# Attention, a gated mixture of experts and a second feed-forward on one core: scatters bound to their steps, ranks behind the next scores, the branch inside the last expert

## The chip, the cores and the metric

The kernel runs on one core of a Trainium2 chip. The metric is the device time of the whole program in microseconds; before the change three runs gave 991.46, 991.9 and 992.49 us. Engines go by the profile's names: PE is TensorE (PEld its weight loads), DVE VectorE, ACT ScalarE, POOL GpSimd, SP SyncE. Each has its own instruction queue and takes it in order; they wait for each other on semaphores.

## What is computed

Three stages in a row, all in float32. First, causal attention in a window of 128 with a linear bias, for 4 batches of 8 heads, 576 positions, head size 64:

```
scores = where(0 <= rel < 128, q @ k.T / 8 - slope[h] * |rel|, -1e9)
attn   = exp(scores - max) / (sum + 1e-9);   x = attn @ v        # 2304 tokens x 512
```

Second, a mixture of 8 experts (512 to 1024 to 512), each token sent to the two with the highest noisy gate value, weighted by a softmax over the two:

```
noisy = x @ w_gate + log1p(exp(x @ w_noise)) * noise;   top2, weights = best two, softmax
out[token] += weight * (relu(x[token] @ w1[e]) @ w2[e])
```

Third, a dense feed-forward on all tokens: `(relu(x @ w_in) ** 2) @ w_out`, 512 to 2048 to 512.

## The kernel before

**Attention.** The 2304 tokens are 18 tiles of 128, the 8 heads two halves: 36 steps. The loop over v (L549 on) runs the scores of step v + 2 (`s_step`), transposes the probabilities of v + 1 (`t_step`) and multiplies by the values for v (`pv_step`, then `norm`). Behind the scores DVE makes four row reductions (L259, each with a read-out of the row maximum, tile mx), then ACT the exponentials. Scores and value products alternate in the two PSUM buffers named b, so a new step's scores wait until the four reductions of the step before have read theirs. Buffer c, of which there is one, is shared by the gate's transposes (L330), its products (L341, L349), the ranks (L384) and some later work.

**The gate, folded in.** Pairs of tiles p = 0 to 8 are gated while attention goes on. A table `todo`, filled by `at(v, slot, f)`, says beside which step and at which place of it a piece runs: slots 0 to 3 stand behind the four reductions of L259, slot 4 behind the transposes, slot 5 behind the value products. For a pair, `gate_t` transposes its tokens, `gate_w` and `gate_m` make the logits, `gate_o` picks the top two (L360 to L374), `rank` counts on PE how many tokens before this one chose the same expert (one-hot times a triangle, plus the running count acc), `place` turns that into a slot number (its first piece is the CAST of L394, which reads the ranks from buffer c), and `scatter` writes token numbers into a table of slots by an indirect DMA on POOL, four to a pair, with a small POOL instruction (the spacer, L424) ahead of each. Three early parts of the table are read by SP (`early_table`, L498) as soon as all tokens that can belong to them are placed; `gather` (L438) then fetches the tokens by an indirect DMA, and `x_in` (L445) transposes them for the first expert, all before attention ends.

**Experts.** Eight experts in a row, each: first layer in two parts (`mm1_a`, 384 columns, and `mm1_b`, 256), second layer `mm2` in five tiles of 128 rows (L787). fp32 products are split into three passes. Weights come through `raw` buffers and are split by ACT, DVE and POOL. Where a token would not fit in its expert's slots, the count `most` is above zero and a slow general path `fallback` is run behind a `tc.If` (L989), which stands between the seventh and the last expert. It isn't taken for these inputs. Each engine reads the flag and branches by itself.

**Behind the last expert.** While it works, sums of second-stage weights are made (L868), and the expert outputs of each token are fetched (`ygather`, L707), weighted and added (`combine`, L713 and L714), and transposed (`x2_in`, L723). A table C_AT says beside which f of the last `mm1_a` they stand, M_AT beside which (j, f) of the last second layer. Then L1040 and L1195 are the dense feed-forward.

## Time and profile before

| | us |
|---|---|
| median of 3 runs (lowest, highest) | 991.9 (991.46, 992.49) |
| the profiled execution | 989.7 |
| its span, first to last instruction | 987.8 |
| PE busy in it | 961.7 |
| DVE, ACT, POOL busy | 672.1, 463.8, 419.0 |

The profile follows one execution. A timeline lists what an engine did with start and duration; matmuls overlap, so one starts before the last has ended, and the distance from start to start says what one costs. In brackets stands the idle time ahead of a row and what ended it. "Granted clock" is PE's clock as a share of full speed; over the whole span it is 0.995.

### The profile page before, as it was taken

The page shows a single profiled execution, that of the slowest core. Times are in us where ns is not written, and L with a number is a line of the kernel's source. Part 1 is how long each engine was busy: PE and PEld are TensorE (multiplying, and loading weights), DVE is VectorE, ACT ScalarE, POOL GpSimd, SP SyncE. Part 2 cuts the span into 40 slices and gives each one's busy share as a digit, 9 for nine tenths or more (in the row PEclk, how much of TensorE's full clock was granted, in tenths as well). Part 3 has the DMA queues.
Part 4 walks back from the last instruction along what each step waited for, and adds up shares of the span by engine and source line. Part 5 has one row for each costly group of instructions (what it writes and reads, how often), then busy time and mean ns, then how long its engine had stood idle before and what let it go on. Part 6 is the DMA issues. An engine that isn't in the chain of part 4 may idle for free. (4 is left out here: it accounts for less than half of the span.)

```text
span 987.8 us, 19656 instructions
## 1 busy us (share of the span) xinstructions
PE 961.7 (97%) x7452; PEld 882.1 (89%) x7452; DVE 672.1 (68%) x1424; ACT 463.8 (47%) x887; POOL 419.0 (42%) x453
## 2 busy tenths in 40 slices
PE   8998999999999999999999799999999999999998
PEld 5776779898998989899898797999999998999998
DVE  4777754657585776857584235778577899877773
ACT  5777743334343433434243336665555564433331
POOL 1564553124233323515243023624212657988880
PEclk9999999999999999999999899999999999999999
DMA  9767625456667575656655352975637874444331
GB/s 324 261 220 265 205 88 153 131 167 224 204 211 225 176 238 199 219 188 215 217 191 171 112 160 87 293 216 168 168 105 211 237 219 139 150 146 132 129 107 43
DMA packets 118199, 180.70 MB, mean 183 GB/s; under 512 B 11104, under 2 KB 66032, under 8 KB 117712
## 3 DMA queue, kind: packets, MB, share of 16 engines
q1 hardware_dynamic: 107120, 147.46, 46.3%
q0 software_dynamic: 10976, 31.90, 10.5%
q8 instruction: 60, 0.98, 0.4%
q14 instruction: 43, 0.35, 0.1%
HBM read 125.02 MB, written 54.30 MB: 182 GB/s over the span
## 5 line engine op out<-in xcount | busy, mean ns | idle before, releaser
L868 POOL TENSOR_TENSOR gs<-xb 128x256 f32<-128x256 f32 x72 | 69.2, 982 | 28.2 <-DVE wc L868 12.6
L473 ACT ACTIVATE ha<-psa 128x384 fp32r<-128x384 f32 x64 | 31.3, 490 | 93.7 <-PE psa L469 92.2
L265 ACT ACTIVATE p<-p,mx 128x192 f32<-128x192 f32 x144 | 57.6, 451 | 31.1 <-DVE mx L259 30.2
L707 POOL DMA_INDIRECT yr<-yg,pos x36 | 36.5, 1012 | 76.5 <-DVE ha L474 50.9
L686 POOL TENSOR_TENSOR et<-ex,et 128x512 f32<-128x512 f32 x16 | 20.8, 1301 | 111.9 <-DVE ex L682 111.9
L474 DVE SCALAR_TENSOR_TENSOR ha<-psa,ha 128x384 fp32r<-128x384 f32 x64 | 35.4, 553 | 46.5 <-ACT ha L473 46.4
L259 DVE CUSTOM_DVE_ANT_0 p<-psb,bias 128x192 f32<-128x192 f32 x144 | 45.8, 352 | 15.6 <-PE psb L254 14.5
L425 POOL DMA_INDIRECT slots<-tok,pos x36 | 35.0, 972 | 44.8 <-DVE rs L311 32.6
L438 POOL DMA_INDIRECT xr<-xd,gidx x40 | 44.7, 1118 | 21.4 <-issue 6.7
L469 PE MATMUL psa<-xa,wa 128*128 128x384 f32 x288 | 53.4, 336 | 0.1
L469 PE MATMUL psa<-xa,wc 128*128 128x384 f32 x288 | 53.1, 335 | 0.0
L787 PE MATMUL psb<-wa,ha 128*128 128x512 f32 x216 | 53.1, 396 | 0.0
L791 ACT ACTIVATE yo<-psb 128x512 f32<-128x512 f32 x38 | 22.7, 597 | 60.5 <-PE psb L787 46.3
L469 PEld LDWEIGHTS psa<-xa,wa 128*128 128x128 f32 x288 | 49.4, 188 | 0.4 <-DVE ha L474 0.3
L469 PEld LDWEIGHTS psa<-xa,wc 128*128 128x128 f32 x288 | 49.6, 188 | 0.2
L868 DVE TENSOR_TENSOR wc<-gs,wc 128x512 fp32r<-128x512 f32 x48 | 48.5, 1050 | 0.0
L882 POOL DMA_DIRECT2D raw<-w x49 | 27.3, 562 | 49.8 <-DVE wb L868 18.4
L686 POOL TENSOR_TENSOR ex<-ex 128x512 f32<-128x512 f32 x12 | 15.6, 1301 | 75.4 <-DVE ex L682 75.4
L787 PEld LDWEIGHTS psb<-wa,ha 128*128 128x128 f32 x216 | 39.5, 188 | 7.8
L787 PE MATMUL psb<-wb,ha 128*128 128x512 f32 x176 | 46.3, 398 | 0.0
L110 DVE TENSOR_TENSOR wa<-raw,wa 128x1024 fp32r<-128x1024 f32 x20 | 25.6, 1279 | 29.6 <-ACT wa L106 29.6
L469 PE MATMUL psa<-xb,wc 128*128 128x256 f32 x288 | 39.6, 294 | 5.2 <-DVEq L989 5.2
(326 smaller groups left out, 2738.2 us busy)
## 6 DMA issues: line engine op xcount, KB each, us to landing
raw<-in_w_dram SPq DMA_DIRECT2D x64, 512.0 KB, 5.0
xb<-gmid SPq DMA_DIRECT2D x72, 256.0 KB, 2.8
v<-in_vt_dram SPq DMA_DIRECT2D x20, 520.0 KB, 4.7
yg<-yo SPq DMA_DIRECT2D x40, 256.0 KB, 3.4
raw<-w POOLq DMA_DIRECT2D x36, 256.0 KB, 3.6
gmid<-yo SPq DMA_DIRECT2D x48, 192.0 KB, 2.7
ex<-in_w_in_dram SPq DMA_DIRECT2D x16, 512.0 KB, 4.1
ex<-in_w_out_dram SPq DMA_DIRECT2D x16, 512.0 KB, 3.6
```

The costliest lines, as they stand in the source:

```text
L259: nc.vector.tensor_tensor_reduce(out=p2[j][:, a, :], in0=ps[:, a, j, :], in1=bias[:, 4 * g + 2 * j + a, :], op0=OP.add, op1=OP.min, scale= ...
L265: nc.scalar.activation(out=p2[j][:, a, :], in_=p2[j][:, a, :], func=AF.Exp, bias=mx[j][:, a:a + 1], scale=-1.0)
L425: st = nc.gpsimd.indirect_dma_start(out=slots, out_offset=bass.IndirectOffsetOnAxis(ap=pos[:, i, k:k + 1], axis=0), in_=tok[:, i:i + 1], i ...
L438: nc.gpsimd.indirect_dma_start(out=XR[e, j], out_offset=None, in_=xd[0:PARTS[j] * 128] if early else xd, in_offset=bass.IndirectOffsetOnAx ...
L469: nc.tensor.matmul(o, w[wp][:, f * 128:(f + 1) * 128], x[:, xp, d, :], start=(n == 0), stop=(n == 11))
L473: nc.scalar.activation(out=hi, in_=ps, func=AF.Relu)
L474: nc.vector.scalar_tensor_tensor(out=lo, in0=ps, scalar=0.0, in1=hi.bitcast(F32), op0=OP.max, op1=OP.subtract)
L686: nc.gpsimd.tensor_tensor(out=x, in0=af, in1=cf, op=OP.add)
L707: nc.gpsimd.indirect_dma_start(out=YR[i, k], out_offset=None, in_=yg, in_offset=bass.IndirectOffsetOnAxis(ap=pos[:, i, k:k + 1], axis=0))
L787: nc.tensor.matmul(py, h[:, hq], wc[wp][:, wsl], start=(f + n == 0), stop=(f == 7 and n == 2))
L868: f(**a)
L882: (nc.sync if m < 15 else nc.gpsimd).dma_start(out=w_buf(m)[:, 0:256 * n_i], in_=w7[kk, :, i:i + n_i, :].rearrange("p i n -> p (i n)"))
```

## The change

- `scatter`: the spacer instruction is now a copy of one element of mx, the row maximum of the step in which it is issued, so it waits for that step's last reduction. Scatters stand one to a step in four steps, two to a step for the late pairs, and all four together for the last pair; before, two to a step in two steps.
- `rank`: from slot 5 of its step to a new slot 6 of the next step, which stands behind that step's score products and ahead of its reductions. `place` is spread over two steps instead of one.
- Early rows: `early_table`, `gather` and `x_in` of the three parts stand at steps 19/20/24, 27/28/32 and 33/34/36, where they stood at 17/18/20, 25/26/28 and 31/32/36; the gather stands in slot 2 instead of 5.
- The branch: from between the last two experts to a place inside the last expert's second layer, behind the first 12 of its 120 products; the path that isn't taken uses other scratch.
- `combine`, `x2_in` and `ygather` of the first three tiles each stand one f earlier.

```diff
--- before.py
+++ after.py
@@ -227,7 +227,7 @@
 
     def s_step(v, now):
         if v >= NV:
-            for n in range(4):
+            for n in (6, 0, 1, 2, 3):
                 run(now, n)
             return
         i, g = divmod(v, 2)
@@ -254,11 +254,13 @@
                     nc.tensor.matmul(ps[64 * x:64 * x + 64, a, j, 192 - n:192],
                                      Q[i][pa, 2 * g + j, 64 * x:64 * x + 64], K[b][pa, 2 * g + j, k0:k0 + n],
                                      start=True, stop=True)
+        run(now, 6)
         for j in range(2):
             for a in range(2):
                 nc.vector.tensor_tensor_reduce(
                     out=p2[j][:, a, :], in0=ps[:, a, j, :], in1=bias[:, 4 * g + 2 * j + a, :],
                     op0=OP.add, op1=OP.min, scale=-0.125, scalar=3.0e38, accum_out=mx[j][:, a:a + 1])
+                G["mx"] = mx[j]
                 run(now, 2 * j + a)
         for j in range(2):
             for a in range(2):
@@ -419,9 +421,9 @@
             nc.vector.tensor_tensor(out=pos[:, two, :], in0=pf, in1=over, op=OP.min)
             del G["gs", p], G["oh", p], G["ri", p]
 
-    def scatter(i):
-        for k in range(2):
-            nc.gpsimd.memset(spacer, 0.0)
+    def scatter(i, *ks):
+        for k in ks:
+            nc.gpsimd.tensor_copy(spacer, G["mx"][0:1, 1:2])
             st = nc.gpsimd.indirect_dma_start(
                 out=slots, out_offset=bass.IndirectOffsetOnAxis(ap=pos[:, i, k:k + 1], axis=0),
                 in_=tok[:, i:i + 1], in_offset=None)
@@ -519,19 +521,18 @@
         o = v + 2 if end else v + 3
         for n, c in enumerate((0, 0, 0, 1, 2)):
             at(o, c, gate_o, p, n)
-        at(o, 4 if end else 5, rank, p)
-        for n, c in enumerate((0, 1, 1, 2, 2, 3)):
-            at(o + 1, c, place, p, n)
-        at(o + 1, 3, scatter, 2 * p)
-        if end or 2 * p + 2 == PARTS[-1]:
-            at(o + 1, 4, scatter, 2 * p + 1)
-        else:
-            at(o + 2, 3, scatter, 2 * p + 1)
+        at(o + 1 - end, 4 if end else 6, rank, p)
+        q = o + (1 if end else 2)
+        for n, c in enumerate((0, 1, 1, 2, 2, 3) if end else (-3, -1, 0, 1, 1, 2)):
+            at(q - (c < 0), c % 4, place, p, n)
+        per = 4 if end else 2 if 2 * p + 2 >= PARTS[-1] else 1
+        for n in range(4):
+            at(q + n // per, 4 if end and n > 1 else 3, scatter, 2 * p + n // 2, n % 2)
     at(0, 3, more_consts)
     at(4, 4, zero_rows)
-    for j, (v, w, x) in enumerate(((17, 18, 20), (25, 26, 28), (2 * PARTS[-1] + 3, 2 * PARTS[-1] + 4, last + 1))):
+    for j, (v, w, x) in enumerate(((19, 20, 24), (27, 28, 32), (2 * PARTS[-1] + 5, 2 * PARTS[-1] + 6, last + 1))):
         at(v, 4, early_table, j)
-        at(w, 5, gather, 0, j, True)
+        at(w, 2, gather, 0, j, True)
         at(x, 5, x_in, 0, j)
     at(last, 5, keep_warm, 24)
     at(last + 2, 3, mm1_a, 0, 0)
@@ -725,8 +726,9 @@
 
 
     def fallback():
-        wb, wt, ex = lay("wb", F32), lay("wt", F32), lay("ex", F32)
-        w = [(wb[:, m * 1024:(m + 1) * 1024], wb[:, (m + 4) * 1024:(m + 5) * 1024] if m < 3 else wt) for m in range(4)]
+        ha, xb, ex = lay("ha", F32), lay("xb", F32), lay("ex", F32)
+        w = [(ha[:, m * 1024:(m + 1) * 1024], ha[:, (m + 4) * 1024:(m + 5) * 1024] if m < 2 else
+              xb[:, (m - 2) * 1024:(m - 1) * 1024]) for m in range(4)]
         xs = ex[:, 0:3072]
         xr, hf = xs[:, 0:512], xs[:, 1024:2048].rearrange("p (f n) -> p f n", f=8)
         xt, yf = xs[:, 512:1024].rearrange("p (c n) -> p c n", c=4), xs[:, 2048:2560]
@@ -985,9 +987,6 @@
                 if j < 4 and nprep[0] < 8 * (e + 1) + 8:
                     prep_one()
 
-    settle("rest")
-    with tc.If(nc.values_load(most[0:1, 0:1], min_val=0, max_val=N) > 0):
-        fallback()
     settle("wb")
     wq = [f for n in range(3) for f in w_sums(n, 0)]
     for f in range(8):
@@ -1003,6 +1002,11 @@
     for j in range(2):
         py = bank("b")[:, 0, :] if j else bank("c")
         for f in range(8):
+            if (j, f) == (0, 4):
+                with tc.If(nc.values_load(most[0:1, 0:1], min_val=0, max_val=N) > 0):
+                    fallback()
+                big["ha"] = lay("ha")
+                settle("rest")
             mm2(last, j, f, py)
             if len(wq) > 8:
                 wq.pop(0)()
@@ -1010,8 +1014,8 @@
     settle("xb")
     for i in range(3):
         ygather(i)
-    C_AT = {5: [(combine, 0)], 6: [(x2_in, 0, "b"), (ygather, 3), (combine, 1)],
-            7: [(x2_in, 1, "b"), (ygather, 4), (combine, 2)]}
+    C_AT = {4: [(combine, 0)], 5: [(x2_in, 0, "b"), (ygather, 3), (combine, 1)],
+            6: [(x2_in, 1, "b"), (ygather, 4), (combine, 2)], 7: [(x2_in, 2), (ygather, 5)]}
     for f in range(8):
         mm1_a(last, f)
         out_a(last, f)
@@ -1019,7 +1023,7 @@
             g(*a)
         wq.pop(0)()
     settle("wc")
-    M_AT = {0: [(x2_in, 2), (ygather, 5)], 1: [(combine, 3)], 2: [(x_hi, 0)], 3: [(x2_in, 3), (x_lo, 0, "dve")], 4: [(combine, 4)], 5: [(x_hi, 1)],
+    M_AT = {1: [(combine, 3)], 2: [(x_hi, 0)], 3: [(x2_in, 3), (x_lo, 0, "dve")], 4: [(combine, 4)], 5: [(x_hi, 1)],
             6: [(x2_in, 4), (x_lo, 1, "dve")], 8: [(combine, 5)], 10: [(x2_in, 5)], 11: [(x_early, 6)],
             12: [(x_early, 5)], 13: [(x_hi, 5)], 14: [(x_early, 3), (x_lo, 5, "dve")], 15: [(x_hi, 3)],
             16: [(x_lo, 3, "dve"), (x_hi, 6)], 17: [(x_early, 4), (x_lo, 6, "dve")], 19: [(x_hi, 4)],
```

PE in attention, pair 2: the products of L300 (values), L384 (ranks), L254 (scores), L276 and L330 (transposes) of one step. Before:

```order
L300 MATMUL psb<-v,pt 64x65 x16
L384 LDWEIGHTS tri
L384 MATMUL psc<-oh,tri 128x8
...
L384 MATMUL psc<-acc,ones 128x8
L254 MATMUL psb<-k,q 64x192 x8
L276 MATMUL psa<-cst,p_1206 128x128 x3
L276 MATMUL psa<-cst,p_1212 128x128 x3
L330 MATMUL psc<-cst,xi 128x128 x4
```

And now, with lines two higher:

```order
L302 MATMUL psb<-v,pt 64x65 x16
L254 MATMUL psb<-k,q 64x192 x8
L386 LDWEIGHTS tri
L386 MATMUL psc<-oh,tri 128x8
...
L386 MATMUL psc<-acc,ones 128x8
L278 MATMUL psa<-cst,p_1202 128x128 x3
L278 MATMUL psa<-cst,p_1208 128x128 x3
L332 MATMUL psc<-cst,xi 128x128 x4
```

The ranks went from ahead of the scores to behind them; everything else of the step keeps its place.

DVE in the same step, from the last part of `norm` on: xi is the attention output, acc the running count, L394 (now L396) the cast that reads the ranks, the L259 pairs (now L260) the reductions. Before:

```order
L317 TENSOR_TENSOR xi<-psb,rs 128x256
L387 TENSOR_TENSOR acc<-acc,oh 128x16 x2
L259 ISA p_1287,mx<-psb,bias 128x192
L259 ISA mx 128x1
L394 CAST ri<-psc 128x16
L259 ISA p_1287,mx<-psb,bias 128x192
L259 ISA mx 128x1
L398 TENSOR_SCALAR ri<-ri 128x16
```

And now:

```order
L319 TENSOR_TENSOR xi<-psb,rs 128x256
L389 TENSOR_TENSOR acc<-acc,oh 128x16 x2
L260 ISA p_1272,mx<-psb,bias 128x192
L260 ISA mx 128x1
L260 ISA p_1272,mx<-psb,bias 128x192
L260 ISA mx 128x1
L396 CAST ri<-psc 128x16
L260 ISA p_1278,mx<-psb,bias 128x192
```

The cast stands behind the second reduction instead of the first, and the rest of `place` went behind the fourth and into the next step.

PE at the branch, which is the pair TENSOR_LOAD and COMPARE_AND_BRANCH (L989, now L1006); wb and wt hold weights of the seventh expert, wa and wc of the last. Before:

```order
L787 MATMUL psb<-wb,hb 128x512 x2
L787 MATMUL psb<-wt,hb 128x512
L787 MATMUL psb<-wb,hb 128x512
L989 TENSOR_LOAD most
L989 COMPARE_AND_BRANCH
...
L989 UNCONDITIONAL_BRANCH x2
L469 MATMUL psa<-xb,wc 128x256 x96
L787 MATMUL psc<-wa,hb 128x512 x24
```

And now:

```order
L789 MATMUL psb<-wb,hb 128x512
L471 MATMUL psa<-xb,wc 128x256 x96
L789 MATMUL psc<-wa,hb 128x512 x12
L1006 TENSOR_LOAD most
L1006 COMPARE_AND_BRANCH
...
L1006 UNCONDITIONAL_BRANCH x2
L789 MATMUL psc<-wa,hb 128x512 x12
L789 MATMUL psb<-wa,hb 128x512 x24
```

The branch went behind the 96 products of the last expert's first layer and the first half of a chain of 24 of its second.

## Rows read from the trace of the kernel before

**Rows 1.** The page's first part: busy time of each engine and its share.

```profile
PE 961.7 (97%) x7452; PEld 882.1 (89%) x7452; DVE 672.1 (68%) x1424; ACT 463.8 (47%) x887; POOL 419.0 (42%) x453
```

**Rows 2.** Timeline of PE, 12 to 66 us: start, duration, instructions, idle before.

```profile
12.08 1.56 PE L254 MATMUL psb<-k,q 64*64 64x192 f32 x16 [2.23 <-DMA q<-in_qt_dram]
...
53.74 1.13 PE L300 MATMUL psb<-v,pt 128*64 128x65 f32 x32
54.69 0.83 PE L254 MATMUL psb<-k,q 64*64 64x192 f32 x16
...
61.48 0.21 PE L384 MATMUL psc<-oh,tri 128*128 128x8 bf16 x2 [0.31 <-DVE oh L372]
...
61.92 0.88 PE L254 MATMUL psb<-k,q 64*64 64x192 f32 x16
...
63.46 0.63 PE L330 MATMUL psc<-cst,xi 128*128 128x128 f32 x4
64.02 1.13 PE L300 MATMUL psb<-v,pt 128*64 128x65 f32 x32
65.17 0.30 PE L243 MATMUL psb<-far,ones 64*64 64x256 bf16 x4
```

**Rows 3.** Timeline of DVE, the same step and the step of 129 us.

```profile
61.69 0.08 DVE L259 DVE_READ_ACCUMULATOR2_ANT mx<- 128x1 f32 x1
...
62.50 0.36 DVE L387 TENSOR_TENSOR acc<-acc,oh 128x16 bf16<-128x16 bf16 x2
62.86 0.36 DVE L259 CUSTOM_DVE_ANT_0 p<-psb,bias 128x192 f32<-128x192 f32 x1
...
63.15 0.17 DVE L394 CAST ri<-psc 128x16 int32<-128x16 f32 x1
...
129.02 0.08 DVE L259 DVE_READ_ACCUMULATOR2_ANT mx<- 128x1 f32 x1
```

**Rows 4.** Timeline of PE, the first early x_in.

```profile
84.37 0.66 PE L445 MATMUL psa<-cst,xr 128*128 128x128 f32 x4 [1.98 <-DMA xr<-xd,gidx]
```

**Rows 5.** Timeline of POOL: two gathers (L438), the last scatter of pair 6 (L425).

```profile
76.10 1.00 POOL L438 DMA_INDIRECT xr<-xd,gidx  x1 [2.32 <-PE psc L384]
...
127.40 0.96 POOL L425 DMA_INDIRECT slots<-tok,pos  x1 [0.22 <-issue]
132.35 0.98 POOL L438 DMA_INDIRECT xr<-xd,gidx  x1 [3.99 <-PE psc L330]
```

**Rows 6.** Timeline of PE: the third early x_in, the first expert's mm1_b.

```profile
136.95 0.60 PE L445 MATMUL psa<-cst,xr 128*128 128x128 f32 x4
...
163.47 11.83 PE L469 MATMUL psa<-xb,wa 128*128 128x256 f32 x96
```

**Rows 7.** Timeline of SP's queue: the third early table.

```profile
129.89 0.33 SPq L498 DMA_DIRECT2D gidx<-slots  x1
```

**Rows 8.** The chain that ended last, 500 to 660 us: start, duration, what.

```profile
587.31 3.74 DMA yr<-yg,pos
```

**Rows 9.** Line 989 by engine queue: durations in ns, first and last start.

```profile
L989 PEldq COMPARE_BRANCH  x1: 5206/5206/5206, 543.4 to 543.4; - x1
...
L989 DVEq COMPARE_BRANCH  x1: 72/72/72, 548.4 to 548.4; - x1
...
L989 DVEq EVENT_SEMAPHORE  x1: 21/21/21, 552.1 to 552.1; - x1
```

**Rows 10.** Timeline of PE, 541 to 600 us.

```profile
541.25 4.70 PE L787 MATMUL psb<-wb,hb 128*128 128x512 f32 x20
...
546.69 0.39 PE L787 MATMUL psb<-wb,hb 128*128 128x512 f32 x1
552.27 14.20 PE L469 MATMUL psa<-xb,wc 128*128 128x256 f32 x96 [5.20 <-DVEq L989]
...
597.35 0.66 PE L723 MATMUL psc<-cst,yr 128*128 128x128 f32 x4 [1.38 <-DVE yr L714]
```

**Rows 11.** Stretch 552 to 556: PE, PEld, DVE, ACT, POOL busy, granted clock, DMA share, GB/s.

```profile
552.00:556.00 4.00, 3.73 (x17) 3.76 (x18) 0.00 (x0) 0.00 (x0) 0.00 (x0) 0.50 0.39 117
```

## The prediction

> **What bounds the kernel now.** I began with the page: PE is busy for 97% of the span [rows 1], every other engine far less. So an edit counts only where it makes or closes a gap on PE, changes PE's clock, or adds work to PE; it adds none. I then read PE's timeline in the three stretches that the change touches, with the bracketed idle times and their releasers: the attention steps (to about 140 us), the branch (547 to 552 us), and the last expert's end (590 to 600 us). DVE, POOL and SP timelines follow each releaser. In attention the bound alternates: PE works through a step of some 3.3 us, and the next scores (L254) need the score buffer, which DVE gives back with the fourth read-out of L259.

> **Rank behind the scores (seven pairs, p = 0 to 6; the other two run where no scores are left).** Before, rank (L384) waits 0.31 us for DVE's one-hot and takes until the scores at 61.92 [rows 2]. It looks as if moving it saves 0.31 + 0.44. But the fourth read-out starts at 61.69 and takes 0.08, to 61.77 [rows 3]: the scores cannot start before it. I put them at 61.83 and gain 0.09. What is late next is the gate transposition (L330, 63.46). PE side: from the scores' start to L330 is 63.46 - 61.92 = 1.54; with rank's 0.40 between (61.48 to 61.92, less a short wait at its end) it would be wanted at 61.83 + 1.54 + 0.40 = 63.77. DVE side: L330 writes the PSUM bank that holds the ranks, so it waits for the CAST (L394) that reads them. The queue of DVE is now acc add, two L259, CAST. The acc add overwrites what rank reads, so it waits for rank's end: scores 61.83 + 0.83 (duration of the scores at 54.69) + 0.40 = 63.06, where before it ran at 62.50, under the scores. Then 63.06 + 0.36 (acc add) + 2 x 0.29 (step from one L259 to the next, 62.86 to 63.15) + 0.17 (CAST) = 64.17. So L330 starts at about 64.2, not 63.46. After it come 0.56 (63.46 to 64.02) and the pv matmuls, 0.95 when nothing holds them (53.74 to 54.69): next scores at 65.71 against 65.17, +0.54. Seven of these: **+3.8**. Ends: if the read-out were not the limit, the 0.31 would go seven times, -2.2; if pv kept its present 1.15 (64.02 to 65.17) as well, 0.74 x 7 = +5.2. I take +3.8, as the wait for the read-out is read from the rows. Place, spread over two steps, has the same instructions; they lie beside PE's work, and if that cover went, the CAST's wait above is the cost, already counted.

> **Early rows later.** The first early x_in (L445, 84.37) waits 1.98 us for its gather [rows 4], issued at 76.10 [rows 5], so 8.27 earlier. It moves four steps behind, its gather only some two: the wait goes, **-2.0** (ends -2.0 and 0). The second had no wait of its own kind and gets more room: 0. The third has less room. Its table needs the scatters of pair 6. Before, POOL issues the last of these at 127.40 and SP reads the table at 129.89, 2.49 later; the gather follows at 132.35, 2.46 later, and x_in runs at 136.95 [rows 5 to 7]. Now each scatter follows a copy of its own step's last row maximum; the last step in question ends its read-out at 129.02 + 0.08 [rows 3], so the last two scatters go at about 129.2 and 130.46 (0.96 of one scatter in its row, and 0.3 that I allow for the next spacer). Table 132.95, gather 135.41, landed some 3.7 later (the gather of 512-wide rows at 587.31 took 3.74 [rows 8]) = 139.1; x_in would have run at 136.95, and gate_w stands behind it in PE's order: **+2.1**. Ends: 0 if the table's 2.49 was mostly queue, +6.7 if the gather lands as late as the first one did, 135.41 + 8.27. Near 137 us the first one's load of weights is gone, so I stay by 3.74.

> The spacer copy stands in place of another one-element POOL instruction, and POOL is busy 42% [rows 1]; of what the scatters write, only the early tables are waited for here: 0 beyond the third table's term.

> **The branch.** No barrier: each engine tests the flag in its own queue. PE's branch instruction stands in the row for 5206 ns, from 543.4 to 548.6, while PE works off what was queued, until 546.69 + 0.39 = 547.07 (5.20 before 552.27). DVE's event comes only at 552.1, and PE starts at 552.27, 5.20 idle [rows 9, 10]. The first matmul behind the branch waited for DVE, since its weights and PSUM come from DVE's work ahead of the branch, and DVE got there last. In the new place the matmuls behind the branch are the second half of a chain of 24 (L787) whose inputs were made long before; only PE's own 5.2 us remain. Queued ahead of the branch PE had 547.07 - 543.4 = 3.6 us; of matmuls of 4.70/20 = 0.23 that is some 16. In the new place these are 12 of L787 (2.76) and four of L469 at 11.83/96 = 0.12 (0.5), 3.2 us [rows 6, 10]. Idle: 5.2 - 3.2 + 0.2 (from DVE's event to the restart, 552.1 to 552.27) = 2.2; with the event's own time I take 2.3, so **-2.9**. Ends: 0 if DVE's event still holds PE, -5.2 if the branch hides altogether. DVE and ACT meet their own branches two relu pairs later, with PE 12 matmuls from needing a PSUM bank; if they stop as long as before (548.4 to 552.1 on DVE), PE has 12 + 24 matmuls of 0.23 to run, 8.3 us, and needs none of them. Its scratch is in other buffers, on a path that isn't taken: 0.

> [...]

> **The clock.** After the gap PE ran at half clock: 0.50 granted from 552 to 556 [rows 11], and the 96 matmuls took 14.20 against 11.83 at full clock (163.47). If the shorter gap doesn't lower it: **-2.4**. A gap of 1.98 at 84.37 left the following x4 at 0.66, while after one of 2.23 at 12.08 the scores took 1.56 instead of 0.83 [rows 2, 4]; the new gap lies between, so this term alone is a case of its own below.

> **Combines one f earlier.** PE waits 1.38 at 597.35 [rows 10] for a combine whose row came at 591.05 (587.31 + 3.74). The transposition now stands a whole f behind its combine; some 0.3 remain for DVE's queue: **-1.1** (0 to -1.4). The gathers start no earlier, since they wait for the results' DMA.

> **Sum:** +3.8 - 2.0 + 2.1 - 2.9 - 2.4 - 1.1 = -2.5. The profiled execution took 989.7 (span 987.8), so 987.2; the median of the runs shown, 991.9, lies 2.2 above it, and the same difference gives **989.4**. With the wider terms pulling apart (rank -1.4, third gather +2, branch and combine 2 each way) its own range is 987.0 to 992.0.

> **Rivals.**
> B, the clock falls again. For it: 2.23 at 12.08. Against: 1.98 at 84.37. It gives the 2.4 back: 991.8.
> C, rank's waits really vanish, because place is also spread and the read-out comes earlier. For it: 0.31 idle at each; against: scores start 0.15 after the read-out [rows 2, 3]. -2.2 in place of +3.8: 983.4.
> D, the branch costs PE nothing. For it, on DVE the branch's own row is 72 ns [rows 9]; against, PE's 5206. The bubble of 2.3 goes as well: 987.1. [...]
> E, slower: the third early gather is late. Place: POOL L438 and x_in around 137 us, gate_w behind it. Price: +6.7 instead of +2.1, 994.0. It decides from the point where the gather lands 3.74 + 2.5 = 6.2 us behind its issue. For it: 8.27 at 76.10. Against: 4.6 at most from 132.35 to 136.95.
> F, the whole stall moves with the branch: DVE still holds PE for 5.2 and the clock falls again, so +5.3: 994.7. Against: those matmuls read nothing that DVE makes behind the branch. It needs DVE's event to be waited for all the same.

> **How the numbers follow.** Chances: A (the sum) 0.40, B 0.18, C 0.08, D 0.10, E 0.14, F 0.10. What a measurement of this kernel can tell from no change is about 0.2%, 2.0 us: faster is below 989.9. A is below it by only 0.5, so of A about 0.24 is faster and 0.15 the same; B is mostly the same; C and D are faster; E and F slower but for a part of each. That gives faster 0.46, same 0.33, slower 0.21. For 8 in 10 the range leaves out C and the upper half of E and F: 985.5 to 994.3.

> **What would show it.** Rank: scores at once behind the fourth read-out, L330 (now L332) with a wait of about 0.5 on DVE's CAST, steps with rank longer by 0.5. First x_in without a wait; third x_in with about 2 us on its gather. Branch: a gap on PE of 2 to 2.5, ended by PE's own sequencer and not by DVE, and matmuls behind it at 0.23. The last expert's L724 without a wait over 0.5. The forecast is wrong if the seven rounds get shorter, if the gap at the branch is 0 or 5, or if the third x_in waits over 5.

## The result, and the profile after

The changed kernel took 1002.1 us (1000.3 to 1005.2, 4 runs) where the kernel before took 991.9 beside it: ratio 1.0114, 95% interval 1.0081 to 1.0148. It is slower, and outside the range I had given. The profiled execution took 1003.4, span 1001.3, against 989.7 and 987.8.

The two halves of the change went opposite ways. The first expert's first product starts at 158.85 instead of 139.81: attention lost 19.0 us, where I had forecast +3.8 - 2.0 + 2.1 = 3.9. From there to the first product of the dense feed-forward it is 628.33 - 158.85 = 469.5 instead of 615.67 - 139.81 = 475.9: 6.4 gained, and 1.9 more than that without a stretch of half clock at its start.

PE in the changed kernel, the step of pair 2 that [rows 2] show of before; start, duration, instructions, idle before:

```profile
66.06 0.88 PE L254 MATMUL psb<-k,q 64*64 64x192 f32 x16 [0.66 <-DVE rs L313]
66.87 0.20 PE L386 MATMUL psc<-oh,tri 128*128 128x8 bf16 x2
...
67.14 0.85 PE L278 MATMUL psa<-cst,p 128*128 128x128 f32 x6
69.75 0.63 PE L332 MATMUL psc<-cst,xi 128*128 128x128 f32 x4 [1.76 <-DVE ri L396]
70.31 1.13 PE L302 MATMUL psb<-v,pt 128*64 128x65 f32 x32
```

The scores do stand at once behind the fourth read-out, which ends at 65.91 (the bracket names L313, which starts with it). Where rank waited 0.31 before, the scores now wait 0.66. L332 does wait for the cast, but for 1.76 and not 0.5. DVE beside it:

```profile
65.83 0.08 DVE L260 DVE_READ_ACCUMULATOR2_ANT mx<- 128x1 f32 x1
...
66.23 0.42 DVE L319 TENSOR_TENSOR xi<-psb,rs 128x256 f32<-128x256 f32 x1
67.32 1.65 DVE L389 TENSOR_TENSOR acc<-acc,oh 128x16 bf16<-128x16 bf16 x2 [0.66 <-PE psc L386]
68.89 0.35 DVE L260 CUSTOM_DVE_ANT_0 p<-psb,bias 128x192 f32<-128x192 f32 x1
...
69.44 0.17 DVE L396 CAST ri<-psc 128x16 int32<-128x16 f32 x1
...
70.08 1.15 DVE L400 TENSOR_SCALAR ri<-ri 128x16 int32<-128x16 int32 x1
71.14 0.16 DVE L401 SCALAR_TENSOR_TENSOR gs<-ri,cst 128x16 f32<-128x16 int32 x1
```

The acc add takes 1.65 where it took 0.36 [rows 3], and L400 1.15 where its twin before took 0.17. POOL at that time:

```profile
66.05 0.17 POOL L426 COPY spacer<-mx 1x1 f32<-1x1 f32 x1 [3.19 <-DVE rs L313]
66.71 0.98 POOL L427 DMA_INDIRECT slots<-tok,pos  x1 [0.49 <-issue]
67.69 1.04 POOL L108 CAST wa<-raw 128x1024 fp32r<-128x1024 f32 x1
68.82 2.37 POOL L110 TENSOR_TENSOR wa<-raw,wa 128x1024 fp32r<-128x1024 f32 x1
```

POOL splits an expert weight (L108, L110). Of the two acc adds in the row the first alone takes 1.45, to 68.77, 0.04 behind POOL's cast (68.73), and L400 ends at 71.23, 0.04 behind L110 (71.19). The reductions of L260, which read PSUM, run beside L110 at their usual 0.35. So it isn't DVE that is slow: some of its instructions are held until POOL's is done. Six of the seven pairs show 1.65 to 1.72; pair 0, where POOL has no split at that time, shows 0.37. The old binding of the scatters kept the two apart: POOL sat waiting for positions while rank and acc ran (5.45 idle ahead of the scatter at 65.47), and split behind the fourth scatter (from 56.51, the scatter at 55.55). Now the scatter is released by the step's last row maximum, and the split's row begins 0.37 after that of the acc add, which comes later than before, behind the scores. What held the acc add in these 0.37 is not shown; rows on POOL are rough.

The third early x_in, against [rows 6], and what follows it:

```profile
155.57 0.66 PE L447 MATMUL psa<-cst,xr 128*128 128x128 f32 x4 [3.57 <-DMA xr<-xd,gidx]
...
158.85 4.19 PE L471 MATMUL psa<-xa,wa 128*128 128x384 f32 x12
```

It waits 3.57, and the clock is half behind it (granted 0.50 from 158.85 to 163.04): 12 products take 4.19, not 2.33. PE at the branch and at the combines, against [rows 10]:

```profile
567.73 11.68 PE L471 MATMUL psa<-xb,wc 128*128 128x256 f32 x96
579.24 2.91 PE L789 MATMUL psc<-wa,hb 128*128 128x512 f32 x12
583.24 3.00 PE L789 MATMUL psc<-wa,hb 128*128 128x512 f32 x12 [1.08 <-PEq L1006]
...
609.57 0.66 PE L724 MATMUL psc<-cst,yr 128*128 128x128 f32 x4
```

The gap is 1.08 and ended by PE's own queue (L1006), the 96 products are back at full clock (granted 1.00 from 567.73 to 579.24), and the transposes wait for nothing. The branch's own rows, durations in ns:

```profile
L1006 PEldq COMPARE_BRANCH  x1: 3932/3932/3932, 579.1 to 579.1; - x1
...
L1006 DVEq EVENT_SEMAPHORE  x1: 21/21/21, 585.8 to 585.8; - x1
```

DVE is through its branch only at 585.8, 2.6 after PE has gone on: nothing behind the branch on PE waits for it in this profile. In after_again, below, PE waits 0.40 for it later, at 594.64.

### The profile page after: what moved, and what is told of

It reads as the page before. It is cut to its first block, busy times and chain, and to the rows that moved or that the text cites. A ratio compares the mean times of both kernels' runs of the same rounds, so it can differ in the third digit from the quotient of the medians.

```text
span 1001.3 us, 19683 instructions
## 1 busy us (share of the span) xinstructions
PE 966.0 (96%) x7452; PEld 885.9 (88%) x7452; DVE 685.9 (68%) x1424; ACT 463.9 (46%) x887; POOL 422.5 (42%) x453
## 5 line engine op out<-in xcount | busy, mean ns | idle before, releaser
L260 DVE CUSTOM_DVE_ANT_0 p<-psb,bias 128x192 f32<-128x192 f32 x144 | 46.2, 350 | 16.1 <-PE psb L254 15.8
L110 DVE TENSOR_TENSOR wa<-raw,wa 128x1024 fp32r<-128x1024 f32 x20 | 25.9, 1295 | 28.1 <-ACT wa L106 28.1
L302 PEld LDWEIGHTS psb<-v,pt 64*64 64x64 f32 (+1 forms) x1056 | 35.1, 144 | 10.9 <-issue 7.9
L302 PE MATMUL psb<-v,pt 64*64 64x65 f32 (+1 forms) x1056 | 42.9, 241 | 0.0
```

Of the source, the lines that this page charges most:

```text
L260: nc.vector.tensor_tensor_reduce(out=p2[j][:, a, :], in0=ps[:, a, j, :], in1=bias[:, 4 * g + 2 * j + a, :], op0=OP.add, op1=OP.min, scale= ...
L302: nc.tensor.matmul(px[64 * x:64 * x + 64, a, j, :], l, r, start=not any(m[:2] == (x, a) for m in mms[:n]), stop=not any(m[:3] == (x, a, j) ...
```

## The experiments

Theory P: DVE's work on SBUF tiles is held while POOL's split runs, and the bound scatters put the split beside rank. Theory R: the new order of rank, acc add, reductions and cast costs that much by itself. The runs fell on chips of two kinds, called the first and the second chip below: on the first the kernel before takes 988.7 to 991.9 (medians), on the second 1015.3 to 1016.9. Behind each expectation stands what was measured: the ratio to the kernel before on the same chip, its 95% interval and, in places, the median.

**The two halves.** att_only is the change without branch and combines; tail_only (twice more as tail_again and tail_third) is the kernel before with these alone:

```
 # tail_only, against the kernel before
-    settle("rest")
-    with tc.If(...): fallback()
+            if (j, f) == (0, 4):      # in the last expert's mm2; fallback on ha, xb
+                with tc.If(...): fallback()
+    C_AT = {4: [(combine, 0)], 5: [(x2_in, 0, "b"), ...
```

> The kernel before with the attention part of the change alone (scatters bound, ranks behind the scores, early rows later); branch and combines stand where they stood. Both theories put the whole loss into attention: its first expert starts 19.0 us later in the changed kernel (158.85 against 139.81), and the part behind the branch gains back some 8.4 (gap 1.08 instead of 5.20, 96 products in 11.68 instead of 14.20, no wait of 1.38 and 0.3 before the transposes). So 991.9 + 19 = about 1011. Rival: the tail's edits lose too, then it is at or under 1002.

Measured: ratio 1.0187 (1.0130 to 1.0244), 1008.7; first expert at 158.62, the acc add at 1.65 to 1.72 in the same pairs.

> The kernel before with the branch inside the last expert and the combines one f earlier, nothing else. If the two parts add up: 991.9 - 4.1 (gap) - 2.4 (half clock) - 1.9 (combines) = 983.5, with a gap of about 1.1 on PE ended by its own queue. Rival: the short gap came from the shifted state of the changed kernel; then a gap of 2.3, as predicted, and 985 to 989.

Measured: 0.9921 (0.9895 to 0.9947), 982.1; a gap of 1.10 and 96 products in 11.68. The halves add up, within the intervals: 0.9921 x 1.0187 = 1.0106 against 1.0114. The loss is attention's alone.

> Before with the tail's edits alone, on the chip of the three others: 0.992 of before on a chip as the first, 0.995 on one as the second, so over rank_prep2 by some 9 us there and under it by some 5 us on the first.

> Before with the tail's edits alone, once more: 8.5 us under the kernel before on either chip (0.9915), as the place of the gain lies far behind the scatters.

Measured: 0.9919 (0.9891 to 0.9948) on the first chip, 0.9948 (0.9913 to 0.9982) on the second. On the first that is 14 us under rank_prep2 and not 5; on the second the medians differ by 2.5 us, and the 8.5 expected lies at the edge of the interval.

**POOL's split moved, binding removed.** prep_later changes one number in the changed kernel, unbound one line:

```
-            if v % 4 == 2 and nprep[0] < 8:
+            if v > 0 and v % 4 == 0 and nprep[0] < 8:      # prep_later
-            nc.gpsimd.tensor_copy(spacer, G["mx"][0:1, 1:2])
+            nc.gpsimd.memset(spacer, 0.0)                   # unbound
```

> The changed kernel, with POOL's split of an expert weight (L108 and L110) issued behind steps 4, 8, ... 32 instead of 2, 6, ... 30, so it no longer runs while rank and the acc add of the next step do. Theory P (DVE's acc add, 1.65 us instead of 0.36 in six of seven pairs, is held while POOL works on its split): acc add back at 0.36, the wait at L332 1.76 -> about 0.5, L400 1.15 -> 0.17, no half clock; about 1002 - 6 x 1.3 - 4 = 990. Theory R (the order rank, acc, two reductions, cast costs that much by itself): wait stays at 1.76 and the time near 1002.

Measured: 1.0083 (1.0051 to 1.0115), 997.9. The rows of pair 2 in it, PE and then DVE:

```profile
67.32 0.63 PE L332 MATMUL psc<-cst,xi 128*128 128x128 f32 x4 [0.48 <-DVE ri L396]
```

```profile
66.17 0.37 DVE L389 TENSOR_TENSOR acc<-acc,oh 128x16 bf16<-128x16 bf16 x2 [0.66 <-PE psc L386]
...
67.64 0.17 DVE L400 TENSOR_SCALAR ri<-ri 128x16 int32<-128x16 int32 x1
```

The holds are gone in all seven pairs and the wait is 0.48 (0.55 in pair 0): P, and not R. The first expert starts at 152.83 instead of 158.85. That a scatter on POOL is not what holds the acc add shows here too: one runs from 65.56 to 66.52, and the acc add beside it takes 0.37. What is left to the order itself: from one step's value products to the next the step of the rank takes 4.79, 4.76 and 4.75 in pairs 1 to 3 against 4.20, 3.97 and 4.16 before, +0.66; the step behind it, which has less of place now, takes 2.95 and 2.79 against 3.47 twice. Over the four steps of pairs 0, 1 and 2 it is +0.25, +0.27 and +0.71, +0.4 on average. But the time fell by only 4 of the 12 forecast, and the intervals of the two kernels overlap. The split meets another DVE instruction where a gather stands ahead of it on POOL (L374, 1.23 instead of 0.18, at 92.93 and 123.86; the scores wait 1.99 and 2.25 there), and the third x_in still waits, 4.59. POOL and then DVE, at the first of these two places:

```profile
91.77 2.35 POOL L110 TENSOR_TENSOR wb<-raw,wb 128x1024 fp32r<-128x1024 f32 x1
```

```profile
91.96 0.24 DVE L367 MAX8 gs<-gs 128x8 f32<-128x8 f32 x2
...
92.93 1.23 DVE L374 TENSOR_TENSOR oh<-iota,sel 128x32 bf16<-128x32 uint32 x1
```

MAX8, which reads one SBUF tile, goes on beside L110 (0.24 for two); L374, which reads two, is held to 94.16, 0.04 behind it. It is the same in all thirteen profiles that have the change's attention with the split on POOL: beside L110, MAX8, FIND_INDEX8 and RECIPROCAL keep their usual time (0.24 for two, 0.16 and 0.18) in each of 136 rows, as does what reads PSUM (L260, L313, L396), while L362, L374, L400 and the acc add are held in every row.

> The changed kernel with the spacer set to zero again instead of copied from the step's row maximum, so scatters go when their positions are there. Theory P: POOL reaches its split earlier and is idle when the acc add comes: acc 0.36, wait at L332 about 0.5, about 990 to 993. Theory R: 1.76 stays in all six pairs, near 1002. A theory B, that the binding costs by holding POOL and the table late: the third early x_in waits less than 3.57, 2 to 3 us faster, acc add still 1.65.

Measured: 1.0068 (1.0043 to 1.0093), 997.3. The acc add is at 0.37 in all pairs, but the scores of the step before now wait 2.2 to 2.7 for DVE in five of them: the split, no longer behind the bound scatter, meets the gate's own arithmetic. The third x_in waits only 0.36, as theory B had it. The acc add moves the way P says and the x_in the way B says; the time stays above P's 990 to 993.

**No split on POOL, and rank back.** In split_off the line is `prep_one("act", "dve")`; rank_back (again as rank_again) has `at(o, 4 if end else 5, rank, p)`. All three ran on the second chip.

> The changed kernel with the eight weight splits of attention on ACT and DVE instead of POOL (no L108/L110 on POOL at all). Theory P: acc add 0.36 and L400 0.17 in all seven pairs, the wait at L332 0.48 in each, as I had predicted for it; DVE works 8 x 1.28 more and ACT 8 x 1.1, which can hold a step's reductions once a split. About 990 to 996. Theory R (the order by itself): 1.76 stays, 1002 or more.

Measured: 1.0082 (1.0053 to 1.0112). Acc add 0.36 and L400 0.17 in all pairs, as P says, but the wait at L332 is 2.44: DVE now does the 1.22 of L110 itself, in its queue ahead of the acc add. My 0.48 forgot that.

> The changed kernel with rank at its old place (slot 5, ahead of the next scores), the rest of the change kept. Theory P (DVE's work on two SBUF tiles is held while POOL runs its split): the acc add now comes right behind norm, about 66.7 in pair 2, before the split begins at 67.7, so 0.36; no wait at L332 over 0.2; L400 behind the fourth reduction still meets the split and is stretched to 1 us or more. 1002 - 6 x 1.76 - some half clock: 988 to 993. Rival S (scatters and split bound together hold whatever DVE does next): the time lost only moves to L400 and to the next scores, 996 to 1002.

> Rank at its old place, split as in the changed kernel, on the chip of the three others. L400 was stretched to 0.3 to 2.0, the acc add once to 2.0: between the changed kernel and the run before this one, 3 to 8 us above the latter.

Measured: 0.9838 (0.9795 to 0.9880) and 0.9857 (0.9814 to 0.9900). L400 is stretched by different amounts (0.28 to 1.97), the acc add once in each (2.00 and 2.33). On the first chip nothing with the change's attention comes under the kernel before by that much; so the second chip needs a cause of its own.

**What the second chip shows.** There the kernels with the order of before have waits on PE for which the profile shows nothing that PE waits for ("issue"), behind four scatters in a row. The kernel before itself has no profile there. From tail_again, PE and then POOL:

```profile
60.90 1.11 PE L300 MATMUL psb<-v,pt 128*64 128x65 f32 x28
62.48 0.25 PE L300 MATMUL psb<-v,pt 64*64 64x65 f32 x1 [0.46 <-issue]
63.19 0.28 PE L300 MATMUL psb<-v,pt 64*64 64x65 f32 x2 [0.47 <-issue]
```

```profile
58.88 0.99 POOL L425 DMA_INDIRECT slots<-tok,pos  x1 [12.01 <-DVE rs L311]
...
62.71 0.96 POOL L425 DMA_INDIRECT slots<-tok,pos  x1 [0.21 <-issue]
```

Over 14 to 165 us such waits sum to 11.3 in tail_again, 11.1 in tail_early1 and 8.3 in tail_early3; on the first chip the kernel before and tail_only have none.

> The changed kernel itself, beside the next three on one chip. In the last four runs the kernel before took 1016.9 where it had taken 991.9, and profiles of its attention there show PE with nothing to issue for 0.4 to 1.1 us at a time, behind each four scatters in a row. If this was that chip: near 1.011 of before on a chip as the first, under 1.00 on one as the second, since here the scatters stand one to a step.

Measured: 0.9928 (0.9898 to 0.9958), 1010.6, with 0.55 of such waits. So the same change is 1.1% slower on one chip and 0.7% faster on another.

> The run before with the four scatters of a pair in one step instead of one to a step in four; nothing else. Theory B (four scatters in a row keep PE's instructions away on the second chip): PE waits of 0.3 to 1.1 us on issue, near 11 us in all between 14 and 165 us, as in the profiles with the order of before there, and 10 to 25 us longer than rank_prep2. Rival Q (the chip is slower for another reason, and the order of before meets it elsewhere): within 3 us of rank_prep2, under 1 us of such waits. On a chip as the first both say no difference.

> Four scatters in a row, again. On a chip as the second: theory B expects PE waits on issue of near 11 us in all and a time 1.0 to 1.02 of before; the rival under 1 us of such waits and 0.99. On a chip as the first: 1.012 as measured, no such waits.

```
-        per = 4 if end else 2 if 2 * p + 2 >= PARTS[-1] else 1
+        per = 4
```

Both fell on the first chip: 1.0119 (1.0084 to 1.0153) and 1.0086 (1.0055 to 1.0118), no wait on issue, but rank waits 2.2 to 2.4 in five pairs, for the same reason as in unbound. No difference had been expected there; burst took 4 us more than rank_prep2. Whether the four scatters in a row cause the second chip's waits was therefore not tested and stays open. The three profiles there with scatters together have 8.3 to 11.3 us of them, five with scatters spread 0.2 to 3.1; that is all.

**The early rows.** tail_early1 is tail_only with (19, 20, 24) for the first part, tail_early3 with all three as changed; soon is rank_prep with place, scatters, table and gather of pair 6 a step earlier.

> The tail's edits (branch, combines) and the first early part of the table alone at steps 19, 20, 24; all else of attention as before. x_in of the first part waited 1.98 in the profile before and 0.71 in that with the tail's edits: the wait goes, 980 to 981.5. Rival: PE is held in that step by something else as well, then 982, as with the tail's edits alone.

> As the run before, but all three early parts at their later steps. The scatters are unbound here, so the last one for the third table stays at about 127. If the third gather's place (step 34) costs by itself: gather at about 134.5, landed 138.2, x_in 1.3 late, 981 to 982.5. If the wait of 3.57 in the changed kernel comes from the bound scatters: no wait here, and 980 to 981.

Measured, on the second chip: 0.9886 (0.9839 to 0.9932) and 0.9960 (0.9929 to 0.9991). In neither does an early x_in wait for its gather. That fits the bound scatters as the cause of the 3.57; the times, with the waits on issue in them, decide nothing.

> The changed kernel with rank at its old place and POOL's split behind steps 4, 8, ... 32. Theory P: no acc add over 0.4, no L400 over 0.2 but where a gather delays POOL, no wait at L332 over 0.2; the rank term of +3.8 falls away too. Attention then loses only the third x_in's 3.5 against the kernel before: 984 to 988 where before takes 991. Rival: steps stay near those of prep_later, 996.

> The changed kernel with rank at its old place and the split behind steps 4 to 32, again, as the reference of the next two. On a chip as the second: 0.9856 of before as measured there, hardly any wait for instructions. On one as the first: theory P 984 to 988 where before takes 991; rival (what is left of the change still loses what the tail gains): 991 to 996.

Measured: 0.9856 (0.9808 to 0.9905) on the second chip, 1.0058 (1.0039 to 1.0078) on the first, the rival there. In rank_prep2 rank waits 0.15 to 0.28 but in two pairs, where POOL's split is late (2.30 and 1.94), and the third x_in waits 2.99.

> rank_prep2 with place and scatters of pair 6 one step earlier, and the third table and gather too (steps 32 and 33). The third x_in waited 4.22 with them later: the gather is issued about 3.3 earlier, so the wait falls to about 1 and the time by 3 us, more if the half clock behind that wait (12 products in 4.19 instead of 2.33) goes as well: 3 to 5 us under rank_prep2. Rival: the wait's end is set by the DMA and not by the step: under 1 us.

Measured: 1.0005 (0.9989 to 1.0021), 5.3 us under rank_prep2; no wait at the third x_in, first expert's 12 products in 2.33. So its place with the half clock costs about that.

> The run soon with the first two gathers one step later (21 and 29), so that they no longer stand ahead of POOL's split in its queue. Theory P: the two waits of 2.24 and 1.75 at rank fall to 0.3, and the half clock behind them goes: 4 to 6 us under soon, 0.995 of before on a chip as the first, 0.980 on one as the second. Rival: the gathers land late, x_in waits, and nothing is gained.

Measured: 0.9977 (0.9956 to 0.9999), and the two waits are still there, 1.96 and 1.81: my reason was wrong. POOL in soon2 shows another:

```profile
86.87 0.97 POOL L427 DMA_INDIRECT slots<-tok,pos  x1 [2.43 <-DMA gidx<-slots]
87.84 1.04 POOL L108 CAST wb<-raw 128x1024 fp32r<-128x1024 f32 x1
88.97 2.35 POOL L110 TENSOR_TENSOR wb<-raw,wb 128x1024 fp32r<-128x1024 f32 x1
```

```profile
89.44 1.92 DVE L362 TENSOR_TENSOR gs<-gs,nz_sb 128x16 f32<-128x16 f32 x1
```

A scatter may not write the table while SP's copy of the early part reads it; that scatter holds the split back by 2.4, and L362 is held to 91.36, 0.04 behind L110's end at 91.32.

On the first chip the version that beats both kernels by the most is tail_only, 0.992. On the second it is at 0.995, which the intervals do not part from the changed kernel's 0.993; rank_back and rank_prep are lower there, 0.984 and 0.986.

## Why the prediction was wrong

**The step that failed** is the rank term, from the sentence that takes the acc add at 0.36 to the one that ends "the CAST's wait above is the cost, already counted", and beside it the sentence that costs the spacer at nothing because POOL is busy for only 42%. The runs showed 1.65 for the acc add in six of seven pairs and 1.76 for the CAST's wait instead of 0.5, because POOL's split ran beside it. It takes both edits, rank behind the scores and the binding: with rank at its old place (rank_back) the acc add is at 0.36 in six of seven pairs, without the binding (unbound) at 0.37 in all. I followed each instruction's order on DVE and what it waits for, and never asked what POOL does while it runs. The row to see it on was in the trace of before, one step ahead of the rows I used. DVE and then POOL, kernel before:

```profile
59.77 0.26 DVE L360 TENSOR_TENSOR gs<-gs,nz_sb 128x16 f32<-128x16 f32 x1
60.07 0.17 DVE L362 TENSOR_TENSOR gs<-gs,psc 128x16 f32<-128x16 f32 x1
```

```profile
57.64 2.36 POOL L110 TENSOR_TENSOR wa<-raw,wa 128x1024 fp32r<-128x1024 f32 x1
```

L360 takes 0.26 where its like takes 0.17, and ends at 60.03, 0.03 behind L110. In the traces here the acc add, L360 (L362 in the changed kernel) and L374, which are held, read two SBUF tiles, and MAX8, which is not, reads one. The holds end 0.02 to 0.04 behind POOL's instruction in the kernel before and in the changed one. L400 reads one tile and is held all the same, 1.15 instead of 0.17; no run here shows why. Nor do the rows show what decides which of the two waits: the acc add's row began 0.37 ahead of the cast's.

**The size of it,** on the way to the first expert: six acc adds x (1.65 - 0.36) = 7.7; the gate's product in the step before pair 0's rank (L362), held to 1.13 at 32.39 by the same split where its twin before took 0.58, about 0.5; half clock behind that rank (granted 0.54 from 37.8 to 40.4), about 1.0; the order itself 7 x 0.4 = 2.8; third x_in 3.6; first x_in -2.0; half clock in the steps behind the ranks of pairs 4, 5 and 6 (granted 0.60 to 0.64; 4.46, 4.31 and 4.47 against 2.9 at full clock, as in pairs 1 to 3) 4.5; 0.5 ahead of step 2. That is 18.6 of 19.0; the other 0.4 I did not trace.

**Rank's order:** the wait was right in kind and size once the hold is away (0.48 against "about 0.5"). I had put place's spread at nothing; it gives back half a microsecond in the next step, so 0.4 a pair and not 0.54. Case C, that rank's waits vanish, was wrong: they went to the scores (0.66).

**Third early row:** +2.1 forecast, 3.57 measured. The gather landed 3.48 behind its issue, near the 3.74 taken; it was issued later than I had it: the last scatter 1.95 behind the first spacer copy of its step (144.78 to 146.73) instead of 1.3, the gather 5.36 behind that (152.09) instead of 4.95; the other 0.5 is that PE was ready sooner, 7.4 behind that step's last read-out instead of 7.9. It is the binding that makes this wait: 0.36 is left of it in unbound. Case E's price (a landing of 8.3) did not come.

**Branch:** the direction and the waiter were right: PE's own queue ends the gap. The size was off, -2.9 forecast and -4.1 measured, since PE's branch took 3.9 and not the 5.2 of [rows 9]. That is luck and not the place: at the old place it took 5206 and, in att_only, 4192 ns; at the new one 3592 to 4032 in seventeen profiles, and 5291 in the run soon. PE in soon, and its branch, with line numbers one higher:

```profile
570.92 4.32 PE L790 MATMUL psc<-wa,hb 128*128 128x512 f32 x12 [2.60 <-PEq L1007]
```

```profile
L1007 PEldq COMPARE_BRANCH  x1: 5291/5291/5291, 565.5 to 565.5; - x1
```

There the gap is 2.60, near the 2.3 forecast, and the clock falls behind it as in case B: granted 0.65 from 571 to 575, the 12 products in 4.32 instead of 3.00. Cases D and F were wrong; the stall neither vanishes nor moves whole.

**Clock:** -2.4 forecast and -2.5 measured behind the branch. What I did not count is that new gaps of 1.5 to 3.6 in attention would lower it there: granted 0.62 from 155 to 160 us. The length of a gap does not settle it alone: behind the waits of 1.76 in pairs 1 to 3 the clock stayed at 1.00, behind those of 1.77 to 1.83 in pairs 4 to 6 it fell to 0.60 to 0.64.

**Combines:** -1.1 forecast, about -1.6 measured: the wait of 1.38 is gone, and from the first of the last expert's 384-column products to the dense feed-forward it is 36.8 instead of 38.5. The prediction misread one row: the combine at 591.05 is the first tile's, and PE waited at 597.35 for the third's, at 596.54. The waits of 0.2 and 0.3 that the expectations above also count are PEld's; PE had none there, and PEld still has them after the change.

## What to carry to other kernels

When an instruction moves on one engine, look at what the other engines do at the new time, and not only at what the instruction waits for: an instruction that takes longer than its like and ends with another engine's is the sign (here 0.26 instead of 0.17, ending 0.03 behind L110). Something bound to a step also fixes when all that is queued behind it runs. And two halves of a change that go opposite ways are worth a run each before they are judged together; here, on the first chip, the half that wins was hidden by the one that loses.
